# Dealing the rows of a tile to the partitions with a stride of sixteen pieces

## The chip, the cores and the metric

The kernel runs on one core of one Trainium2 chip. The metric is the time of one execution on the device, in microseconds (us). The kernel before was run again beside every experiment on the same chip. A run that is over 1.5% above the fastest of its kernel is called slow, and a single run of a kernel has an unknown state. Ratios are computed as the mean time of one kernel's fast runs over the mean of the other's fast runs in the same rounds, so they are not quite the ratio of the medians quoted next to them.

## The reference

The input is an image of 384 x 384 positions with 384 channels in bf16. The function averages each channel over all positions, multiplies by one weight, takes the sigmoid, and scales the channel with it.

```python
def reference(x, w1d):                       # x: (1, 384, 384, 384), w1d: (1,)
    B, H, W, C = x.shape
    g = jnp.einsum("bhwc->bc", x) / (H * W)
    s = _sigmoid(g * w1d[0])                 # cut: padding and loop, empty for k = 1
    return x * s[:, None, None, :]
```

The image is 113.25 MB. It must be read once and written once, 226.5 MB in all, if the scale is known before the rest of the image has left the chip's memory again.

## The kernel before

The kernel estimates the scale from the first 1,024 positions (`FIRST` = 8 rows per partition), scales and stores every tile with this estimate at once, sums everything on the side, and checks at the end that the true scale has the same bf16 bits. A second pass, which these inputs never need, would repair a wrong estimate. So loads and stores run together nearly all the time.

A tile is 44 rows per partition. One row is 384 channels, 768 bytes. So a tile is 128 *pieces* of 44 neighbouring rows, and a piece is 33,792 bytes, without a gap in memory. Partition p takes piece p:

```python
FIRST, TILE, SLOTS, BOTH = 8, 44, 6, 3

    def dram(view, r0, n):
        return view[r0 * P : (r0 + n) * P, :].rearrange("(p t) c -> p (t c)", p=P)
    ...
    def load(place, n, r0, queues=("sync",)):
        i = 0
        for queue, m in zip(queues, split(n, -(-n // len(queues)))):
            plan.dma(
                queue,
                at(place + i, m),
                dram(x_rows, r0, n)[:, i * C : (i + m) * C],
                writes=rows(place + i, m),
            )
            i += m
    ...
    def put(place, n, r0):                    # scale on VectorE, then store
        plan.op("vector", gate(place, place, n, s_early), ...)
        plan.final.append(
            plan.dma("scalar", dram(o_rows, r0, n), at(place, n), reads=rows(place, n))
        )
    ...
    for k in range(n_tiles):                  # 26 tiles, 6 slots of SBUF
        if k >= SLOTS:
            put(slot(k), TILE, row0(k - SLOTS))
            load(slot(k), TILE, row0(k))      # waits for the store from this slot
```

Loads are issued on SyncE's queue (SP, q1 in the profile), stores on ScalarE's (ACT, q10). The first three tiles are loaded in two column halves, one on each queue. The sums (matmuls with a matrix of ones) and the scaling treat all positions alike, so they do not care which piece lies in which partition, as long as load and store agree.

## Time and profile before

| | before |
|---|---|
| median of three runs | 532.62 us (531.38 to 539.72) |
| span of the profiled run | 530.8 us |
| TensorE busy, VectorE busy | 47%, 45% |
| DMA, 13 to 500 us | 426 to 433 GB/s at a busy share of 1.00 to 1.02 |
| 33,792-byte packets | 97.8% of 6,272 take 1.26 us or less, nearly all 1.251 us |

First the table of stages of the kernel before. Its columns are the stretch and its length, the busy time of each engine with the number of instructions (PE is TensorE and PEld its weight loads, DVE is VectorE, ACT ScalarE, POOL GpSimd), the granted TensorE clock, the busy share of the 16 DMA engines, and the rate that they moved.

```profile
core 0: us, PE busy (x) PEld busy (x) DVE busy (x) ACT busy (x) POOL busy (x), PEclk, DMA share, GB/s
13.00:30.00 17.00, 12.47 (x49) 0.00 (x0) 4.78 (x2) 0.00 (x0) 0.00 (x0) 0.80 1.01 431
30.00:60.00 30.00, 21.19 (x85) 0.00 (x0) 24.87 (x4) 0.00 (x0) 0.00 (x0) 0.85 1.02 426
60.00:200.00 140.00, 66.26 (x231) 0.00 (x0) 63.59 (x8) 0.00 (x0) 0.00 (x0) 0.70 1.00 432
200.00:400.00 200.00, 94.59 (x330) 0.00 (x0) 88.31 (x11) 0.00 (x0) 0.00 (x0) 0.72 1.00 432
400.00:500.00 100.00, 48.30 (x168) 0.00 (x0) 43.26 (x6) 0.00 (x0) 0.00 (x0) 0.73 1.01 433
```

The share of 1.00 to 1.02 says that the DMA engines are busy all the time, and the rate says what that busy time is worth. The stretch 13 to 30 us moves almost only loads, the later ones loads and stores mixed, and both run at about 432 GB/s, which is 16 engines x 33,792 bytes / 1.251 us. The compute engines are half idle (TensorE is busy 47%, VectorE 45%). So the bound is DMA.

The DMA rows of the page for the kernel before, over 40 equal slices of the span:

```profile
DMA  8999999999999999999999999999999999999996
GB/s 360 429 435 402 446 435 423 438 430 428 443 418 438 441 418 441 441 420 438 430 428 441 420 438 443 418 441 438 425 438 425 433 443 415 441 441 420 442 430 299
```

The rate is flat but for the first and the last slice. From the same page come the DMA issues (the last column is the median time from issue to landing), and from its list of groups comes the scaling on VectorE (busy us, mean ns of one, idle us before it):

```profile
out_dram<-arena ACTq DMA_DIRECT2D x26, 4224.0 KB, 64.5
arena<-in_x_dram SPq DMA_DIRECT2D x23, 4224.0 KB, 37.4
arena<-in_x_dram SPq DMA_DIRECT2D x3, 2112.0 KB, 23.4
L201 DVE TENSOR_TENSOR arena<-arena,s_early 128x16896 bf16<-128x16896 bf16 (+1 forms) x27 | 234.5, 8691 | 262.9 <-PE acc L237 262.2
```

One tile of 4,224 KB alone would take about 10 us at 432 GB/s, an estimate from the table of stages. The 37 and 64 us to landing are therefore read as mostly waiting behind other transfers; the DMA share of 1.00 agrees.

### The profile page before, as it was taken

The page shows a single profiled execution, that of the slowest core. Times are in us where ns is not written, and L with a number is a line of the kernel's source. Part 1 is how long each engine was busy: PE and PEld are TensorE (multiplying, and loading weights), DVE is VectorE, ACT ScalarE, POOL GpSimd, SP SyncE. Part 2 cuts the span into 40 slices and gives each one's busy share as a digit, 9 for nine tenths or more (in the row PEclk, how much of TensorE's full clock was granted, in tenths as well). Part 3 has the DMA queues.
Part 4 walks back from the last instruction along what each step waited for, and adds up shares of the span by engine and source line. Part 5 has one row for each costly group of instructions (what it writes and reads, how often), then busy time and mean ns, then how long its engine had stood idle before and what let it go on. Part 6 is the DMA issues. An engine that isn't in the chain of part 4 may idle for free. (4 is left out here: it accounts for less than half of the span.)

```text
span 530.8 us, 1113 instructions
## 1 busy us (share of the span) xinstructions
PE 247.2 (47%) x871; PEld 0.2 (0%) x2; DVE 241.1 (45%) x45; ACT 2.7 (1%) x4; POOL 0.3 (0%) x6
## 2 busy tenths in 40 slices
PE   3669274274363263372472472562461561562600
PEld 0000000000000000000000000000000000000000
DVE  3096924614624615615516516426516416426360
ACT  1000000000000000000000000000000000000000
POOL 0000000000000000000000000000000000000000
PEclk9798675775786876876876765766876867866855
DMA  8999999999999999999999999999999999999996
GB/s 360 429 435 402 446 435 423 438 430 428 443 418 438 441 418 441 441 420 438 430 428 441 420 438 443 418 441 438 425 438 425 433 443 415 441 441 420 442 430 299
DMA packets 8358, 226.53 MB, mean 427 GB/s; under 512 B 931, under 2 KB 931, under 8 KB 1315
## 3 DMA queue, kind: packets, MB, share of 16 engines
q10 hardware_dynamic: 4466, 120.13, 52.5%
q1 hardware_dynamic: 3888, 106.37, 46.8%
q8 instruction: 1, 0.02, 0.0%
q14 instruction: 3, 0.02, 0.0%
HBM read 113.25 MB, written 113.25 MB: 427 GB/s over the span
## 5 line engine op out<-in xcount | busy, mean ns | idle before, releaser
L237 PE MATMUL acc<-arena,ones 128*128 128x512 bf16 x863 | 244.7, 454 | 247.5 <-PEq L276 247.5
L201 DVE TENSOR_TENSOR arena<-arena,s_early 128x16896 bf16<-128x16896 bf16 (+1 forms) x27 | 234.5, 8691 | 262.9 <-PE acc L237 262.2
L309 DVE TENSOR_TENSOR total<-total,acc 128x128 f32<-128x128 f32 (+2 forms) x11 | 4.5, 407 | 0.3
L390 ACT ACTIVATE arena<-total,w_scaled 128x384 bf16<-128x384 f32 x1 | 0.6, 614 | 499.4 <-DVE total L309 499.4
L335 PE MATMUL w_all<-w_one,ones 1*128 1x1 bf16 x1 | 0.2, 158 | 4.7 <-DMA w_one<-in_w1d_dram 4.7
L237 PE MATMUL acc<-zeros,ones 128*128 128x512 bf16 x6 | 2.3, 507 | 0.0
L307 DVE COPY total<-acc 128x384 f32<-128x384 f32 x1 | 0.6, 558 | 3.3 <-PE acc L237 3.3
L344 DVE TENSOR_SCALAR w_scaled<-w_all 128x1 f32<-128x1 f32 x2 | 0.2, 152 | 3.9 <-PE w_all L335 3.9
L329 ACT ACT_TABLE_LOAD x1 | 1.3, 1283 | 3.8 <-issue 3.8
L235 PE MATMUL acc<-arena,ones 128*128 128x512 bf16 x1 | 0.6, 586 | 0.8 <-DMA arena<-in_x_dram 0.8
L398 DVE TENSOR_TENSOR total<-arena,s_early 128x384 f32<-128x384 uint16 x1 | 0.6, 559 | 0.7 <-ACT arena L390 0.7
L366 ACT ACTIVATE s_early<-total,w_scaled 128x384 bf16<-128x384 f32 x1 | 0.6, 614 | 5.9 <-DVE total L309 5.9
L406 DVE TENSOR_REDUCE wrong<-total 128x1 f32<-128x384 f32 x1 | 0.6, 553 | 0.0
L353 DVE MEMSET ones<- 128x128 bf16 x1 | 0.2, 165 | 0.8 <-PEq L493 0.8
L329 ACT ACTIVATE warm<-warm 128x1 f32<-128x1 f32 x1 | 0.2, 203 | 0.0
L412 DVE CAST redo<-wrong 128x1 int32<-128x1 f32 x1 | 0.2, 153 | 0.0
L235 PEld LDWEIGHTS acc<-arena,ones 128*128 128x128 bf16 x1 | 0.1, 103 | 0.9 <-DMA arena<-in_x_dram 0.9
L493 POOL MEMSET const-bfloat16-1.0<- 128x1 bf16 x1 | 0.1, 102 | 0.0
L493 POOL MEMSET const-uint8-127<- 128x1 uint8 x1 | 0.1, 102 | 0.0
L335 PEld LDWEIGHTS w_all<-w_one,ones 1*128 1x128 bf16 x1 | 0.1, 100 | 4.7 <-issue 4.7
L352 POOL MEMSET zeros<- 128x2 bf16 x1 | 0.1, 100 | 0.0
L351 POOL MEMSET warm<- 128x1 f32 x1 | 0.1, 99 | 0.3 <-POOLq L493 0.3
(2 smaller groups left out, 0.2 us busy)
## 6 DMA issues: line engine op xcount, KB each, us to landing
out_dram<-arena ACTq DMA_DIRECT2D x26, 4224.0 KB, 64.5
arena<-in_x_dram SPq DMA_DIRECT2D x23, 4224.0 KB, 37.4
arena<-in_x_dram SPq DMA_DIRECT2D x3, 2112.0 KB, 23.4
arena<-in_x_dram ACTq DMA_DIRECT2D x3, 2112.0 KB, 24.4
out_dram<-arena ACTq DMA_DIRECT2D x1, 768.0 KB, 38.3
arena<-in_x_dram ACTq DMA_DIRECT2D x1, 384.0 KB, 4.8
arena<-in_x_dram SPq DMA_DIRECT2D x1, 384.0 KB, 4.7
w_one<-in_w1d_dram ACTq DMA_DIRECT2D x1, 0.0 KB
```

Of the source, the lines that this page charges most:

```text
L201: return lambda e: e.tensor_tensor(to_v, v, s_b, ALU.mult)
L235: loaded.append(e.matmul(bank, weights, moving, start=start, stop=stop))
L237: return e.add_instruction(mybir.InstMatmult(name=nc.get_next_instruction_name(), engine=mybir.EngineType.PE, ins=[e.lower_ap(moving), e.l ...
L307: emit = lambda e, part=part, of=of: e.tensor_copy(part, of)
L309: emit = lambda e, part=part, of=of: e.tensor_tensor(part, part, of, ALU.add)
L329: lambda e: e.activation(warm[:, 1:2], warm[:, 0:1], ACT_F.Sigmoid),
L335: lambda e: e.matmul(w_all[:, 0:1], ones[0:1, :], w_one[0:1, 0:1], start=True, stop=True),
L344: lambda e, i=i, n=n: e.tensor_scalar_mul(w_scaled[:, i : i + 1], w_all[:, 0:1], 1.0 / float(P * n)),
L366: lambda e: e.activation(s_early[:], total[:], ACT_F.Sigmoid, scale=w_scaled[:, 0:1]),
L390: lambda e: e.activation(s_true, total[:], ACT_F.Sigmoid, scale=w_scaled[:, 1:2]),
L398: lambda e: e.tensor_tensor(total[:], s_true.bitcast(U16), s_early[:].bitcast(U16), ALU.not_equal),
L406: lambda e: e.reduce_max(wrong[:], total[:], axis=mybir.AxisListType.X),
```

## The change

The intent is locality: pieces that the 16 DMA engines move at the same moment shall lie closer together in memory. The memory side of each transfer gets the order (e, j) with 16 values of e outermost and 8 of j inside, and partition 8e + j takes piece 16j + e. So partitions that lie eight apart take neighbouring pieces. That such pieces are moved at the same moment is the intent.

```diff
+    def plain(view, r0, n):
+        return view[r0 * P : (r0 + n) * P, :].rearrange("(p t) c -> p (t c)", p=P)
+    ENGINES = 16
     def dram(view, r0, n):
-        return view[r0 * P : (r0 + n) * P, :].rearrange("(p t) c -> p (t c)", p=P)
+        return view[r0 * P : (r0 + n) * P, :].rearrange(
+            "(j e t) c -> e j (t c)", e=ENGINES, j=P // ENGINES
+        )
@@ in load
-                dram(x_rows, r0, n)[:, i * C : (i + m) * C],
+                dram(x_rows, r0, n)[:, :, i * C : (i + m) * C],
```

(The second pass, which never runs here, keeps the old order through `plain`.) The memory side now has three dimensions, the SBUF side still 128 partitions. No byte, instruction or semaphore is added.

More of the change, by code (lines that the diff above doesn't have):

```diff
@@ L422, in bass_standalone__channel_attn_eca__vision_kernel @@
         place = k % 2 * half
-        again.dma("sync", at(place, n), dram(x_rows, r0, n), writes=rows(place, n))
+        again.dma("sync", at(place, n), plain(x_rows, r0, n), writes=rows(place, n))
         again.op(
@@ L430, in bass_standalone__channel_attn_eca__vision_kernel @@
         again.final.append(
-            again.dma("scalar", dram(o_rows, r0, n), at(place, n), reads=rows(place, n))
+            again.dma("scalar", plain(o_rows, r0, n), at(place, n), reads=rows(place, n))
         )
```

## The prediction

> **What bounds the kernel now.** The DMA engines. In the 40-slice view the DMA row is 9 (90% or more) in all but the first and last slices; the table of stages gives a DMA share of 1.00 to 1.02 from 13 to 518 us, at 426 to 437 GB/s, also in the load-only stretch 13 to 30 us (431 GB/s). PE is busy 47% and DVE 45% of the span; SP's own waits put 440 us on earlier stores. In the packet records 98% of the 33,792-byte packets take 1.251 us: 27.0 GB/s per engine, 432 for sixteen. 226.5 MB at that rate are 524 us; start and last landing are the other 7. So the memory side shows no slack that locality could give back: packet time above 1.251 us sums to about 27 us over 16 engines, under 2 us each, and the lag of the last engines in a tile's landings (4.3 us at the end) is 0.8%. Under 522 us is all but excluded.
>
> **What the change does.** No byte, instruction or semaphore is added or removed: still 128 pieces of 33,792 bytes a tile. The sums and the gate don't care which row lies in which partition; load and store use the same order. The memory side's outermost dimension becomes 16 in place of 128[...]. [...]
>
> **Cost, an estimate.** [...]720 us, range 528 to 1000. Chances: faster 0.02, same 0.40, slower 0.58.
>
> **What would show it.** Right: same packets and bytes; durations of the 33,792-byte packets split, many near 2.5 us already in 13 to 30 us, where GB/s falls to about half; DMA share near 1.0 while GB/s falls to 230 to 350; single PE and DVE instructions unchanged, their idle time longer; time to landing up by the same factor. Wrong: packets stay at 1.251 us and 432 GB/s; [...]locality was worth nothing because each engine was already at its rate.
>
> **What would make it wrong.** [...]pieces are cut smaller.

The sum had two branches: 700 to 1000 us, from 500 us of mixed stage times a guessed factor of 1.3 to 1.9 plus a start of twice its length, and 530 to 535 us if nothing changes. The point of 720 us lies between the two.

## The result and the profile after

The changed kernel took 680.75 us in the median of four runs (671.43 to 699.47; the two over 681 us count as slow) against 532.0 us before (530.81 to 539.72). The ratio of the fast runs is 1.268, with a 95% interval of 1.255 to 1.282. The profiled run is a fast one with a span of 669.9 us. The result is correct.

The table of stages of the changed kernel, with the columns of before:

```profile
13.00:30.00 17.00, 0.23 (x1) 0.00 (x0) 2.99 (x4) 0.61 (x1) 0.00 (x0) 0.60 1.01 226
30.00:60.00 30.00, 18.23 (x65) 0.00 (x0) 10.33 (x2) 0.00 (x0) 0.00 (x0) 0.77 1.00 225
60.00:200.00 140.00, 55.42 (x194) 0.00 (x0) 56.73 (x7) 0.00 (x0) 0.00 (x0) 0.70 1.00 325
200.00:400.00 200.00, 84.48 (x291) 0.00 (x0) 79.37 (x10) 0.00 (x0) 0.00 (x0) 0.69 1.00 385
400.00:500.00 100.00, 38.49 (x129) 0.00 (x0) 41.69 (x5) 0.00 (x0) 0.00 (x0) 0.68 1.00 390
500.00:640.00 140.00, 49.72 (x165) 0.00 (x0) 48.49 (x14) 0.61 (x1) 0.00 (x0) 0.63 1.00 333
640.00:660.00 20.00, 0.00 (x0) 0.00 (x0) 0.00 (x0) 0.00 (x0) 0.00 (x0) 0.50 0.72 226
660.00:670.00 10.00, 0.00 (x0) 0.00 (x0) 0.00 (x0) 0.00 (x0) 0.00 (x0) 0.50 0.16 54
```

The DMA rows, the issues and the scaling of the changed kernel:

```profile
DMA  9999999999999999999999999999999999999983
GB/s 208 223 224 228 226 286 335 323 335 393 389 361 381 416 359 381 377 412 377 373 377 422 381 377 383 404 387 365 383 400 371 365 351 325 319 339 281 314 258 113
out_dram<-arena ACTq DMA_DIRECT2D x26, 4224.0 KB, 79.9
arena<-in_x_dram SPq DMA_DIRECT2D x23, 4224.0 KB, 37.1
arena<-in_x_dram SPq DMA_DIRECT2D x3, 2112.0 KB, 41.0
L210 DVE TENSOR_TENSOR arena<-arena,s_early 128x16896 bf16<-128x16896 bf16 (+1 forms) x27 | 234.7, 8692 | 371.5 <-PE acc L246 370.9
```

Three things are to be seen. First, the busy share is still 1.00 to 1.01 up to 60 us while the rate is about half (225 to 226 GB/s): the share counts the whole duration of a packet, and from 13 to 30 us a packet on SP's queue takes 2.38 us in place of 1.26 us (table below). Second, the loss is a factor of 1.9 where almost only loads run (226 against 431 GB/s), then recedes to 11% of the rate (385 against 432), then grows at the end. Third, one scaling takes 8692 ns as before; only its idle time grew.

A count over the packet records of the traces (packets of 16,896 bytes are scaled to 33,792) shows the same, by queue:

```
kernel  stretch us   queue  packets  mean us  share <=1.26  1.26-1.6  1.6-2.2  >2.2 us
before   13 to 30    SP      223     1.260       77%          23%       0%      0%
after    13 to 30    SP      112     2.383        0%           0%       0%    100%
before  200 to 400   SP     1276     1.255       98%           1%       0%      0%
after   200 to 400   SP     1140     1.520       42%          29%      20%      9%
before  200 to 400   ACT    1281     1.252       99%           1%       0%      0%
after   200 to 400   ACT    1141     1.290       68%          31%       0%      0%
```

Where the 139 us between the two spans went can be added up in two ways. By packets: all packet time divided by 16 engines is 527.5 us before and 656.9 us after, so 129 us are longer packets, and the other 10 us are engines that finish at different times. The 16 completions of the last store span 4.3 us before and 29.5 us after. By stages, an estimate that takes the missing bytes at 432 GB/s: about 27 us in the first 60 us, 35 us from 60 to 200, 32 us from 200 to 500, and the remaining 46 us after that.

### The profile page after: what moved, and what is told of

It is laid out like the page before. It is cut to its first block, busy times and chain, and to the rows that moved or that the text cites. A ratio compares the mean times of both kernels' runs of the same rounds, so it can differ in the third digit from the quotient of the medians.

```text
span 669.9 us, 1096 instructions
## 1 busy us (share of the span) xinstructions
PE 250.7 (37%) x854; PEld 0.2 (0%) x2; DVE 241.3 (36%) x45; ACT 2.7 (0%) x4; POOL 0.3 (0%) x6
## 5 line engine op out<-in xcount | busy, mean ns | idle before, releaser
L246 PE MATMUL acc<-arena,ones 128*128 128x512 bf16 x846 | 248.3, 461 | 352.8 <-PEq L285 350.3
L210 DVE TENSOR_TENSOR arena<-arena,s_early 128x16896 bf16<-128x16896 bf16 (+1 forms) x27 | 234.7, 8692 | 371.5 <-PE acc L246 370.9
L244 PE MATMUL acc<-arena,ones 128*128 128x512 bf16 x1 | 0.6, 587 | 0.0
## 6 DMA issues: line engine op xcount, KB each, us to landing
out_dram<-arena ACTq DMA_DIRECT2D x26, 4224.0 KB, 79.9
arena<-in_x_dram SPq DMA_DIRECT2D x23, 4224.0 KB, 37.1
```

The lines of the kernel that those rows point to most:

```text
L210: return lambda e: e.tensor_tensor(to_v, v, s_b, ALU.mult)
L244: loaded.append(e.matmul(bank, weights, moving, start=start, stop=stop))
L246: return e.add_instruction(mybir.InstMatmult(name=nc.get_next_instruction_name(), engine=mybir.EngineType.PE, ins=[e.lower_ap(moving), e.l ...
```

## The experiments

The theory under test is that the loss goes with the outermost size of 16, wherever the pieces lie, and that it comes from the parts of a transfer running in step. Where an expectation gives two sets of figures, those before the word "rival" belong to this theory. Three rivals are: the closeness itself (neighbouring pieces collide in memory), the third dimension of the transfer (it is slow by itself), and a milder form of the theory (a transfer with 16 outermost is slow as such, in step or not).

### 1. Close pieces with 32 outermost

```diff
 # against the changed kernel
-    ENGINES = 16
+    ENGINES = 32
```

Four consecutive partitions now take pieces 32 apart, and partitions four apart take neighbouring pieces. The transfer has three dimensions as in the change.

> The memory side has 32 pieces outermost in place of 16: four consecutive partitions take pieces that lie 32 apart. [...]the transfer still has three dimensions on the memory side. [...]98% of the 33,792-byte packets take 1.25 us, load-only stretch 13 to 30 us at 430 GB/s, time 529 to 536 us. Rival (close pieces collide in memory, or a three-dimensional transfer is slow by itself): packets of about 2.4 us in the load-only stretch and 650 to 700 us.

It measured 529.89 us (529.82 to 529.95, four runs) against 536.75 us before on the same chip, ratio 0.988 (0.982 to 0.994). Two stages of this run:

```profile
13.00:30.00 17.00, 12.23 (x44) 0.00 (x0) 4.27 (x2) 0.43 (x1) 0.00 (x0) 1.00 1.01 432
200.00:400.00 200.00, 94.13 (x330) 0.00 (x0) 90.77 (x11) 0.00 (x0) 0.00 (x0) 0.72 1.00 433
```

The rate is back at 432 GB/s with close pieces and with three dimensions. The third dimension falls as the cause of the loss. So does closeness in this form, with the neighbouring pieces in partitions four apart in place of eight; experiment 2 tests it from the other side. One number, 16 or 32, makes the difference. The run is also a little faster than the kernel before, which experiments 5 to 7 take up.

### 2. 16 outermost without the closeness

```diff
 # against the changed kernel, full tiles only
+        if n == TILE:
+            k = (r0 - FIRST) // TILE
+            start = FIRST + k // 2 * 2 * TILE
+            both = view[start * P : (start + 2 * TILE) * P, :].rearrange(
+                "(e h j t) c -> h e j (t c)", e=ENGINES, h=2, j=P // ENGINES
+            )
+            return both[k % 2, :, :, :]
```

Two tiles now share a region of 256 pieces, and each outermost entry takes eight neighbours in it.

> 16 outermost as in the change, [...]as slow as the change, 650 to 710 us, load-only packets about 2.4 us, 210 to 230 GB/s in 13 to 30 us. Rival (closeness in memory is what hurts): 530 to 540 us.

It measured 687.9 us (685.48 to 703.97), ratio 1.281 (1.272 to 1.291).

```profile
13.00:30.00 17.00, 1.47 (x4) 0.00 (x0) 4.26 (x7) 0.61 (x1) 0.00 (x0) 1.00 1.01 226
200.00:400.00 200.00, 77.49 (x272) 0.00 (x0) 80.63 (x9) 0.00 (x0) 0.00 (x0) 0.69 1.00 377
```

Without the closeness the same 226 GB/s appear. So the loss goes with 16 outermost, not with where the pieces lie.

### 3 and 4. The kernel before, with loads or stores cut into partition halves

A transfer of 64 partitions asks whether the loss can come without the new memory order and without a third dimension.

```diff
 # halved loads, against the kernel before
-            plan.dma(queue, at(place + i, m), dram(x_rows, r0, n)[:, i*C:(i+m)*C], ...)
+            for h in range(2):
+                plan.dma(queue, at(place + i, m)[64*h : 64*h+64, :],
+                         dram(x_rows, r0, n)[64*h : 64*h+64, i*C:(i+m)*C],
+                         writes=rows(place + i, m, (h,)))
 # halved stores: the same in put(). Both: 92 semaphores for transfers in place of 70.
```

> The kernel before with its row order and two-dimensional transfers; only each load is cut into two, partitions 0 to 63 and 64 to 127, one after the other on the same queue, stores as before. [...]load-only packets take about 2.5 us and 13 to 30 us shows about 216 GB/s; stores stay near 1.25 us; time 570 to 720 us. Rival (the slowdown needs the new row order or the third dimension): packets stay at 1.25 us, 530 to 540 us.

> The mirror of the run with halved loads: loads as before, each store cut into two partition halves. [...]430 GB/s in the load-only stretch, store packets up to 2.5 us where loads and stores run together and in the last stores, time 560 to 720 us.[...]

Why half of the partitions should be slower was not shown. Cut with it is the other outcome for the halved stores: 530 to 545 us with store packets at 1.25 us if the stores lose nothing by it.

Halved loads took 653.49 us (648.51 to 658.45), ratio 1.215 (1.204 to 1.226). Halved stores took 572.1 us (three fast runs at 567.66 to 572.23, one slow at 620.93), ratio of the fast runs 1.064 (1.056 to 1.072). First two stages of the run with halved loads, then the DMA rows of the run with halved stores (whose profile fell on the slow run, so only rates inside one stage are read from it):

```profile
13.00:30.00 17.00, 2.72 (x7) 0.00 (x0) 4.29 (x7) 0.61 (x1) 0.00 (x0) 1.00 1.03 234
200.00:400.00 200.00, 74.84 (x266) 0.00 (x0) 73.56 (x9) 0.00 (x0) 0.00 (x0) 0.68 1.00 388
```

```profile
DMA  8999999999999999999999999999999999997941
GB/s 366 432 437 400 393 417 373 380 362 384 373 395 388 410 395 402 404 384 388 415 393 397 410 386 380 412 393 410 404 340 402 388 351 375 360 367 206 218 99 37
```

Halved loads reproduce the picture of the change almost stage by stage (234 and 388 against 226 and 385 GB/s). The load-only packets of SP average 2.35 us, and none is under 1.6 us. The row order is the old one, so limiting each transfer to half the partitions is enough for nearly the whole loss (ratio 1.215 against 1.268). A rival is that two transfers per tile are slow as such. The kernel before speaks against it: its first three tiles are loaded in two halves too, cut by columns and put on two queues, and run at 431 GB/s. The same cut on one queue was not run.

With halved stores the start is at full rate (434 GB/s from 13 to 30 us). Near the end only stores are left (the last load packet ends at 553.6 us), and two slices run at 206 and 218 GB/s. In the first of them the DMA share is only in the 0.7s, so idle engines lower its rate too; in the second, with a share of 0.9 or more, the store packets take 2.63 us in the median. So stores of half the partitions slow down too, as the loads do. The profile is of a slow run, but the fast profiled run of the change has a milder form of it: from 602 to 640 us it has only stores left, and it moves 301 GB/s at a share of 1.01, with packets of 1.81 us on average. The two expectations held, that of the stores at the low end of its range.

### 5 to 7. Does closeness or the form of the transfer give the last per cent?

Experiment 1 beat the kernel before slightly, and this could be the locality that the change was after. Three more kernels vary distance and form. The distance given here is that in pieces between what partition p and partition p + 4 take; which pieces really move at one time no trace shows. The first has 32 outermost but takes its pieces from a region of two tiles as in experiment 2, which makes the distance 8 in place of 1. The second has 64 outermost (distance 2). The third is two-dimensional like the kernel before (distance 4) but with a distance of 8, through `"(p h t) c -> h p (t c)"` with h = 2 in the two-tile region.

> 32 outermost ([...]three dimensions)[...]. If the 1.2% that the run with 32 close pieces gained over the kernel before came from closeness: this run shows the kernel before's late packets at the tile borders again (excess over 1.25 us of 20 us or more in sum, spread of landings growing to 4 us or more) and 531 to 542 us. If it came from the three-dimensional form of the transfer: every packet 1.25 us and 529 to 531 us as with 32 close pieces.

> 64 outermost: [...]529 to 536 us, packets 1.25 us. If closeness pays, 529 to 531 us with hardly any late packet; if it has to be exactly adjacent, like the kernel before.

> The kernel before with two-dimensional transfers, but each partition's pieces two apart in a region of two tiles[...]. If the 0.6% of the three runs with 32 or 64 outermost comes from the three-dimensional form of the transfer: late packets and 531 to 540 us like the kernel before. If it comes from the distance in memory (4 pieces, 132 KiB, being the bad one): every packet 1.25 us and 529 to 531 us.

| kernel | form | distance, p to p + 4 | runs, us | ratio to before (95%) |
|---|---|---|---|---|
| before | 2-D | 4 | 530.77 to 540.6 over all rounds | 1 |
| 32, close | 3-D | 1 | 529.82 to 529.95 | 0.988 (0.982 to 0.994) |
| 64 | 3-D | 2 | 529.69 to 530.1 | 0.994 (0.989 to 0.999) |
| 32, apart | 3-D | 8 | 529.69 to 530.0 | 0.994 (0.989 to 0.998) |
| 2-D, apart | 2-D | 8 | 532.54 to 532.92, and three slow at 540.76 to 542.1 | 0.996 (0.986 to 1.005) |

The first ratio is from another chip than the next two, and the last from a third one. All three-dimensional versions with 32 or 64 outermost agree within 0.4 us at any distance, and at the same distance of 8 the two-dimensional one scatters like the kernel before. So closeness gave nothing that these runs can show. What goes with the gain of about 3 to 7 us, and with the lost scatter, is the form. That this is the cause rests on one kernel on another chip: the ratio 0.996 of the two-dimensional apart version does not tell it from 0.994, only its times (532.54 us and more, against at most 530.1) and its late packets do. In the packet records the time above 1.251 us sums to 27.8 us before and 29.5 us in the two-dimensional apart version, against 10.1 to 11.6 us in the three with three dimensions. The difference lies after the first 60 us: there the excess is 15.2 us before, mostly in bursts about 20 us apart, the time of one tile, against 1.9 us with 32 close pieces. The completions of the last store span 4.3 us before and 1.4 us with 32 close pieces. Over 16 engines the excess differs by only 1 us, and the one trace kept of the kernel before is of a quick run (532.31 us), so its scatter up to 540 us is in no trace. Why the two-dimensional form has such late packets was not found. It is not a faster issue: a load's issue instruction takes longer in the better version, 535 against 328 ns in the median. The kernel before and experiment 1 (min/median/max in ns, then first and last start in us):

```profile
L109 SPq DMA_DIRECT2D arena<-in_x_dram x27: 327/328/877, 0.7 to 451.7; - x27
```

```profile
L109 SPq DMA_DIRECT2D arena<-in_x_dram x27: 534/535/727, 0.7 to 451.5; - x27
```

The 32-outermost version beats both kernels, by 0.6% (apart, chip of experiments 5 and 6) to 1.2% (close) over the kernel before. It is the one to keep.

### 8 and 9. Putting the parts out of step: a first try and its control

If the loss needs the sixteen parts of a transfer to run in step, delays that differ between them should heal the load-only stretch, with the memory order of the change untouched. For this two extra transfers are put ahead, one with 4 and one with 12 outermost entries, which are meant to hold up some engines longer than others. The traces show 5 and 13 updates of their two semaphores (one at once, then 4 and 12 completions), where a full tile has 16 completions; which engines they ran on no run here shows. The expectations call these entries engines. In this first try the transfer with 12 entries has two packets per entry in place of four.

```diff
 # against the changed kernel; BOTH = 0, so full tiles load on SP's queue alone
+    for place, engines, packets in ((5, 4, 4), (4, 12, 2)):   # control: ((5, 16, 4),)
+        n = engines * packets
+        plan.dma("sync", at(slot(place), TILE)[0:n, :],
+            x_rows[0 : n * TILE, :].rearrange("(j e t) c -> e j (t c)", e=engines, j=packets),
+            writes=rows(slot(place), TILE))
```

> The changed kernel, all full tiles loaded on one queue, with two small loads of unused data put ahead on 4 and on 12 engines[...]. [...]load-only stretch 15 to 40 us at 380 to 432 GB/s with most packets at 1.25 us[...]; after the stores start, gain uncertain, total 560 to 670 us. Rival[...]: 225 GB/s and 2.4 us packets as in the change.

> Control of the run with the lag: the same loads on one queue, with one small load ahead[...]. Both theories: as the change, load-only stretch 215 to 230 GB/s with packets of about 2.4 us, total 670 to 710 us.

The lag took 669.61 us and the control 671.19 us, one run each. The expectation for the load-only stretch was missed (the total lies just inside its range of 560 to 670 us): 13 to 20 us ran at 188 GB/s, 20 to 30 us at 248 and 30 to 40 us at 344, against 217, 226 and 259 in the control. The extra loads write into SBUF (the on-chip memory that holds the tiles) themselves. The packets of this stretch were slow (2.1 us on average from 15 to 35 us), and the extra loads landed as late as 19.1 and 26.3 us, against 11.5 and 17.2 us for the transfers of experiment 10. So the test seems badly built rather than negative; that the extra loads and the tiles held each other up was not shown.

### 10 and 11. The lag again, without touching SBUF

```diff
 # against the changed kernel; BOTH = 0
+    at0 = row0(last) * P
+    for name, engines in (("spare0", 4), ("spare1", 12)):     # control: (("spare0", 16),)
+        n = engines * 4 * TILE
+        there, here = (
+            v[at0 : at0 + n, :].rearrange("(j e t) c -> e j (t c)", e=engines, j=4)
+            for v in (o_rows, x_rows))
+        plan.dma("sync", there, here, writes=[name])           # the last store waits for these
+        at0 += n
```

> The run with the lag again, with a delay that writes nothing into SBUF: the extra transfers on 4 and on 12 engines, four packets each, go from memory to memory (into rows of the output that the last store overwrites)[...]. [...]from about 15 us on, load-only packets mostly at 1.25 us and 380 to 432 GB/s in 15 to 35 us, against 2.4 us and 217 to 226 GB/s in the control and in the change; later stages uncertain, total 560 to 675 us. Rival[...]: 2.4 us packets and 220 to 260 GB/s.

> Control of the run with the lag from memory to memory: the same bytes moved ahead from memory to memory (16 engines with 4 packets each in place of 4 and 12 engines)[...]. If the lag and not the extra transfer freed the load-only stretch: 15 to 35 us again at 215 to 235 GB/s with packets of about 2.4 us, total 660 to 700 us. If the extra transfer as such did it: about 414 GB/s and 600 us.

The lag took 601.97 us and its control 669.25 us, one run each, state unknown. The control moves the same extra bytes. Stages of the run with the lag, then of the control:

```profile
15.00:35.00 20.00, 5.55 (x14) 0.00 (x0) 0.00 (x0) 0.00 (x0) 0.00 (x0) 0.50 1.01 414
200.00:400.00 200.00, 89.22 (x310) 0.00 (x0) 80.63 (x9) 0.00 (x0) 0.00 (x0) 0.70 1.00 403
560.00:600.00 40.00, 0.00 (x0) 0.00 (x0) 9.00 (x10) 0.61 (x1) 0.00 (x0) 0.51 0.77 212
```

```profile
15.00:35.00 20.00, 1.78 (x5) 0.00 (x0) 1.76 (x1) 0.43 (x1) 0.00 (x0) 0.55 1.01 234
200.00:400.00 200.00, 81.71 (x287) 0.00 (x0) 77.61 (x9) 0.00 (x0) 0.00 (x0) 0.70 1.00 373
```

The kernel became 67 us faster than its control, with the same bytes moved; what was changed is that the extra ones go as transfers with 4 and 12 outermost entries in place of one with 16. The lag is in the trace: the 16 completions of the first full tile lie 11.6 us apart, against 1.3 us in the control. From 15 to 35 us, 71% of the load packets take 1.26 us or less, against none in the control. The two ran on different chips, but the kernel before took 531 to 540 us on the one and 538.67 us on the other, so 67 us are far beyond what the chips differ by. A transfer with 16 outermost is therefore not slow as such: from 15 to 35 us it runs at 414 GB/s with its completions 11.6 us apart, and at 234 GB/s in the control with 1.3 us. The last line of the run with the lag shows the price that remains: at the end, with only stores left, the rate is 212 GB/s at a DMA share of 0.77.

One limit of this test: the trace does not name a packet's engine. So it shows that the completions are spread and the packets fast, but not which engines were late, nor which of them hold each other up in the change.

## Why the prediction was right

**The bound.** Right. DMA was the bound before, and every experiment's time followed the packet durations (529.89 us at 432 GB/s in the load-only stretch of experiment 1, 687.9 us at 226 GB/s in experiment 2). Nothing fell under 522 us; the best kernel took 529.7 us.

**The cause.** Right in its effect. The hardware reason that the prediction gave was not shown here. What the runs show is this: the loss follows the outermost size and not the closeness of the pieces (226 GB/s with 16 in experiment 2, 432 with 32 in experiment 1), transfers of half the partitions do the same with the old order (234 GB/s, experiment 3), and most of the load-only loss goes away when the completions of a tile are spread in time (414 against 234 GB/s, experiments 10 and 11).

**The size in the load-only stretch.** Right: packets near 2.5 us and about half the rate were named, and 2.38 to 2.44 us and 226 GB/s were measured.

**The size in the mixed stage.** This term was mis-sized. The factor on 500 us of mixed stage was put at 1.3 to 1.9, a guess. Measured by the rates it is 1.33 from 60 to 200 us (432 over 325 GB/s), 1.12 from 200 to 400 us (432 over 385), and 1.30 from 500 to 640 us (432 over 333). A part of the prediction named what makes it smaller, that engines drift out of step. This fits the landing records: the 16 completions of one tile lie 1 to 3 us apart while the rate is 226 GB/s and 5 to 6 us apart, four to five packets of 1.25 us, from about 140 to 400 us, where it is near 385. Which engines drift is not shown, and after 400 us the spread goes on growing (29.5 us for the last store) while the rate falls again, so drift alone does not explain the end.

**Luck.** The branch that came true, the loss, had been put at 700 to 1000 us, and both fast runs, 671.43 and 677.01 us, lie below it. The point of 720 us came near because it was a compromise with the other branch, 530 to 535 us, and "same" had a chance of 0.40. The range of 528 to 1000 us covered both outcomes and excluded hardly anything. That the load-only rate would halve was foreseen; the closeness of the total is in part luck.

**The signs.** Packets and bytes were equal, the DMA share stayed near 1.0, and single instructions stayed the same, as said. One was off: the rate was to fall to 230 to 350 GB/s, and it was 385 to 390 GB/s from 200 to 500 us. And one failed: the time to landing did not grow by one factor. It went from 23.4 to 41.0 us for the first half-tile loads on SP, from 64.5 to 79.9 us for stores, and stayed at 37.4 and 37.1 us for the full loads. A time to landing includes the wait behind other transfers (37 us in the kernel before, against about 10 us for the bytes alone by the estimate above); how that wait changed was not taken apart.

**No slack for locality.** Right for locality: distances of 1, 2 and 8 pieces gave the same time within 0.4 us. But there was a little slack that goes with the memory-side form. The prediction had put the lag of the last engines at 0.8%; the gain was 0.6% on one chip and 1.2%, more than that, on another, with fewer late packets and not from closeness.

## What to carry to other kernels

The outermost dimension on the memory side can change the rate of a transfer even when bytes, packets and the partitions in SBUF stay the same. Here 32, 64 and 128 gave 430 to 432 GB/s in the load-only stretch, and 16 gave 226; why was not shown. So after reordering the memory side, measure that stretch against the old order, and if it lost, try another outermost size. Look at the rate and at packet durations and not at the DMA busy share, since here the share stayed at 1.00 while the rate halved (431 to 226 GB/s). And where 98% of the packets already took 1.26 us or less, as here, an idea about the other end of the transfer had little to win: 0.6 to 1.2%, and not by closeness.
